# Decay attention with a softplus feed-forward layer on one core: from unit 9 on, scores follow the preceding unit's outputs in one TensorE event

## The chip, the cores and the metric

The kernel runs on one core of a Trainium2 chip. The metric is the device time of one execution in microseconds (us); for the kernel before, the median of three runs is 615.9 us (612.82 to 615.99). Profiles are of one execution each, taken by the hardware profiler; their times count from the first instruction of the span.

## The reference

The first half is causal linear attention with a decay for each head, in blocks of 64 positions; the second half is a feed-forward layer with softplus, and no residual connection.

```
B, H, S, D = 4, 8, 768, 64; block = 64
for b in range(S // block):                       # q, k, v of this block: qb, kb, vb
    intra = (qb @ kb.T * Dmask) @ vb              # Dmask[i, j] = lam ** (i - j) for i >= j, else 0
    inter = (qb * lam ** (pos + 1)) @ kv_state
    out[b] = intra + inter
    kv_state = lam ** block * kv_state + (kb * lam ** (block - 1 - pos)).T @ vb
x = out as (3072 tokens, 512)
h = x @ w_in                                      # 512 -> 2048
y = softplus(h) @ w_out                           # 2048 -> 512
```

## The kernel before

**Tiling of the attention.** The sequence is cut into six chunks (NCH) of 128 positions, two blocks of 64. The heads are cut into four pairs (NP). A *unit* g is one chunk and one pair, with all four batches: 24 units, g = 4c + p. Its q, k and v come in one buffer of 8 KB a partition, att, by two loads on the queue of SyncE (`load_upto`, L80). Keys and queries lie there twice where both layouts are needed; k and v are stored back to front in a block, so the decay products need no more than a scale for each row.

A unit has two bursts of small fp32 matmuls, all 64 by 64, four of which sit beside each other in the array:

- *scores* (`scores_of`, L428, `mm_scores`, L289): the products of k and q into one PSUM bank (x, L299) and the contribution of the decayed keys and v to the state into another (y, L301); 64 matmul records. VectorE then masks x (`mask_scores`, L323, L326) and updates the states from y with four instructions (`update_states`, L353, L331).
- *outputs* (`mm_out`, L307): state times decayed query (L314) and v times masked scores (L318) into a two-bank tile z; 64 records. ScalarE then takes the high half of the result (`x_high`, L361, L363) and VectorE the low half (`x_low`, L368, L370): x is kept as a sum of two rounded parts, and each product of the feed-forward layer takes three matmuls.

Ahead of the scores ScalarE makes the decayed keys (`k_decay`, L269, L277) and VectorE the decayed queries (`q_decay`, L279, L284).

**The feed-forward layer.** A chunk has 512 tokens. Its work is cut into 16 slices f of the hidden 2048. For a step s = 16c + f the first layer (`mlp1`, L389, L398) accumulates twelve matmuls 128x512 into one of two PSUM banks of tag "h"; ScalarE takes softplus of it and rounds it, VectorE takes the rest (`chain_act`, `chain_hi`, `chain_lo`, L377 to L387); and four steps later (LAG) the second layer (`mlp2`, L403, L415) adds twelve matmuls into the four banks of tag "o" of that chunk. At a chunk's last step the four banks are copied out (L421) and stored (L423).

**PSUM.** Eight banks: four of tag "o", two of tag "h", and one two-bank tile of tag "t" (`work`, L66), which scores (x and y) and outputs (z) use in turn.

**SBUF.** A pool of 21 buffers of 8 KB ("b8", L48) holds loaded units, raw weights, converted weights (16 for the rest of the run), x and the output tiles. A pool of four buffers of 2 KB ("b2", L54) holds, from unit 4 on, the decayed keys and queries and the masked scores.

**What sets the order.** The schedule is manual: each engine executes its instructions in the order in which the program traces them. The first steps are a list written out by hand (L453 to L463). Then a loop over s runs from 4 to 99 (L473 to L509). In a step, the decay products of a unit whose scores come in the next step stand first, then softplus of step s-1, weight conversion while there is any, then on TensorE the second layer of step s-4, the scores of a unit if `scores_at` has one for this step, the outputs of a unit if `outs_at` has one, and the first layer of step s; and at the end loads, on SyncE's queue. Units 4 to 7 have their scores at steps 3, 6, 9 and 12, units 8 to 23 at steps 17, 21, ... 77, each with its outputs two steps later:

```
scores_at = {3 * n + 3: NP + n for n in range(NP)}
scores_at.update({4 * n + 1 + NF: 2 * NP + n for n in range(NG - 2 * NP)})
outs_at = {s + 2: g for s, g in scores_at.items()}
```

At the end of a step with scores of unit g, `load_upto(g + 2)` issues the load of unit g+1, which waits until a buffer is free.

**The diagonal.** In the first chunk the state passes from one block to the next through a matmul with a diagonal matrix (`carry_states`, L342, L346), kept in a tile of its own, `diag` (L181). The set-up buffer `spare` (L131), one of the 21, holds the ramps from which masks and powers are made, among them `begins` (L149).

Of the kernel before, what the change touches and what calls it, by code (L numbers as in the profile page):

```python
# [7 lines left out]
F32 = mybir.dt.float32  # L8
# [6 lines left out]
B, H, S, D = 4, 8, 768, 64  # L15
C = 128
T = 64
NCH = S // C
NP = H // 2
NG = NCH * NP  # L20
DM = H * D
DFF = 2048
NF = DFF // 128
LAG = 4
# [7 lines left out]
def decay_attention_softplus_ffn(  # L32
# [7 lines left out]
    nc = tc.nc  # L40
    ctx.enter_context(tc.manual_schedule())
    cp = ctx.enter_context(tc.tile_pool(name="cp", bufs=1))
    sb = ctx.enter_context(tc.tile_pool(name="sb", bufs=2))
# [8 lines left out]
        return sb.tile(shape, dt, tag="b4", bufs=7, name=name)  # L52

    def t2(shape, dt, name):  # L54
        return sb.tile(shape, dt, tag="b2", bufs=4, name=name)

    def tl(shape, dt, name):
        return sb.tile(shape, dt, tag="bl", bufs=1, name=name)
# [7 lines left out]
    def work(name):  # L66

        return ps.tile([128, 2, 512], F32, tag="t", bufs=1, name=name)

    def bank(name):  # L70
        return ps.tile([128, 512], F32, tag="h", bufs=2, name=name)
# [8 lines left out]
    def load_upto(n):  # L80
        for g in range(len(units), min(n, NG)):
            t = t8([128, 2, 2, 512], F32, f"att{g}")
            for major in range(2):
                nc.sync.dma_start(out=t[:, major], in_=att[g // NP, g % NP, :, major])  # L84
            units.append(t)

    def part(g, major, kind):
        return units[g][:, major, kind].rearrange("q (b t d) -> q b t d", b=B, t=2)
# [7 lines left out]
    def kt_of(g):  # L96
        return part(g, 1, 0)

    def vt_of(g):
        return part(g, 1, 1)  # L100


    w_order = [(f, 0) for f in range(LAG)]
# [41 lines left out]
    for s in range(2):  # L145
# [7 lines left out]
        out=begins[0], in_=ramp.rearrange("q (o i) -> q o i", o=1).broadcast_to([128, H, T]), scalar=0.0,  # L153
# [24 lines left out]
    nc.gpsimd.iota(  # L178
        off[half(1)], pattern=[[1, T]], base=0, channel_multiplier=-1, allow_small_or_imprecise_dtypes=True
    )  # L180
    diag = cp.tile([128, H, T], F32, name="diag")  # L181
    nc.vector.scalar_tensor_tensor(
        out=diag[half(1)], in0=off[half(1)].rearrange("q (o i) -> q o i", o=1).broadcast_to([64, H, T]), scalar=0.0,
        in1=lam_c[half(1)].rearrange("q (h o) -> q h o", o=1).broadcast_to([64, H, T]),
# [84 lines left out]
    def k_decay(g):  # L269
        kd = kds[g] = own(g, 0, "kd")  # L270
        if g == 0:
            w = rp1[:, heads(g)].rearrange("q (o t w) -> q o t w", o=1, w=1).broadcast_to([128, B, 2, D])
            nc.vector.tensor_mul(out=kd, in0=kt_of(g), in1=w)
            return
        for t in range(2):
            h = heads(g).start + t
            nc.scalar.activation(kd[:, :, t], kt_of(g)[:, :, t], AF.Copy, scale=rp1[:, h : h + 1])  # L277

    def q_decay(g):  # L279
        qd = qds[g] = own(g, 1, "qd")  # L280
        r = hi if first_chunk(g) else slice(0, 128)
        eng = nc.gpsimd if g < 2 else nc.vector
        w = lp[r, heads(g), :].rearrange("q (o t) i -> q o (t i)", o=1).broadcast_to([r.stop - r.start, B, 2 * T])
        eng.tensor_mul(  # L284
            out=qd[r].rearrange("q b t i -> q b (t i)"), in0=q_of(g)[r].rearrange("q b t i -> q b (t i)"), in1=w
        )


    def mm_scores(g, x, y):  # L289
        q, k, kd, v = q_of(g), k_of(g), kds.pop(g), vt_of(g)  # L290
        if first_chunk(g):

            nc.tensor.matmul(y[lo], lhsT=warm[hi, :64], rhs=warm[hi], start=True, stop=False)
        for b in range(B):
            for t in range(2):
                cols = slice((2 * b + t) * 64, (2 * b + t + 1) * 64)
                for s in range(2):
                    r = half(s)
                    nc.tensor.matmul(x[r, cols], lhsT=k[r, b, t], rhs=q[r, b, t], start=True, stop=True)  # L299
                    if s == 0 or not last_chunk(g):  # L300
                        nc.tensor.matmul(  # L301
                            y[half(1 - s), cols], lhsT=kd[r, b, t], rhs=v[r, b, t],
                            start=s == 0 or not first_chunk(g), stop=s == 0 or not first_chunk(g),
                        )


    def mm_out(g, w):  # L307
        a, qd, v, st = aa.pop(g), qds.pop(g), vt_of(g), states[g]
        for b in range(B):
            cols = slice(b * 64, b * 64 + 64)  # L310
            for s in range(1 if first_chunk(g) else 0, 2):
                r = half(s)
                for t in range(2):
                    nc.tensor.matmul(w[half(t), s, cols], lhsT=st[r, b, t], rhs=qd[r, b, t], start=True, stop=False)  # L314
            for s in range(2):
                r = half(s)
                for t in range(2):
                    nc.tensor.matmul(  # L318
                        w[half(t), s, cols], lhsT=v[r, b, t], rhs=a[r, b, t],
                        start=s == 0 and first_chunk(g), stop=True,  # L320
                    )

    def mask_scores(g, x):  # L323
        a = aa[g] = own(g, 2, "a")
        m = mask[:, heads(g), :].rearrange("q (o t) i -> q o t i", o=1).broadcast_to([128, B, 2, T])
        nc.vector.tensor_mul(out=a, in0=x.rearrange("q (b t i) -> q b t i", b=B, t=2), in1=m)  # L326
# [26 lines left out]
    def update_states(g, y):  # L353
        u = y.rearrange("q (b t e) -> q b t e", b=B, t=2)
        st = states[g]
        decayed(g, st[hi], st[lo], lo, u[hi])
        if not last_chunk(g):
            states[g + NP] = th([128, B, 2, D], F32, f"st_{g + NP}")
            decayed(g, states[g + NP][lo], st[hi], hi, u[lo])

    def x_high(g, w):  # L361

        nc.scalar.copy(  # L363
            out=x_of(g // NP, g % NP)[:, 0].rearrange("q (b s i) -> q s b i", b=B, s=2),
            in_=w[:, :, 0:256].rearrange("q s (b i) -> q s b i", b=B),
        )

    def x_low(g, w):  # L368
        x = x_of(g // NP, g % NP).rearrange("q n (b s i) -> q n s b i", b=B, s=2)
        nc.vector.tensor_sub(  # L370
            out=x[:, 1], in0=w[:, :, 0:256].rearrange("q s (b i) -> q s b i", b=B), in1=x[:, 0]
        )
# [30 lines left out]
    def mlp2(ss):  # L403
        c = ss[0] // NF
        ends = ss[-1] % NF == NF - 1
        if ss[0] % NF == 0:
            o_tiles[c] = [obank(f"o{c}_{b}") for b in range(B)]
        if ends:
            ob = t8([128, B, 512], F32, f"ob{c}")
        for b in range(B):  # L410
            for s in ss:
                f = s % NF
                g, w = g_tiles[s], w_of(f, 1)
                for n, (i, j) in enumerate(((0, 0), (0, 1), (1, 0))):
                    nc.tensor.matmul(  # L415
                        o_tiles[c][b], lhsT=g[:, i, b * 128 : (b + 1) * 128], rhs=w[:, j],
                        start=f == 0 and n == 0, stop=f == NF - 1 and n == 2,
                    )
            if ends:
                copy = nc.vector.tensor_copy if b % 2 else nc.scalar.copy  # L420
                copy(out=ob[:, b], in_=o_tiles[c][b])  # L421
                queue = nc.scalar if c == NCH - 1 and b % 2 == 0 else nc.sync
                queue.dma_start(out=out[b * S + c * C : b * S + (c + 1) * C, :], in_=ob[:, b])  # L423
# [4 lines left out]
    def scores_of(g):  # L428
        w = work(f"w{g}")
        mm_scores(g, w[:, 0], w[:, 1])  # L430
        mask_scores(g, w[:, 0])
        update_states(g, w[:, 1])


    xy, z = {}, {}
# [30 lines left out]

    last = NCH * NF
    scores_at = {3 * n + 3: NP + n for n in range(NP)}  # L470
    scores_at.update({4 * n + 1 + NF: 2 * NP + n for n in range(NG - 2 * NP)})
    outs_at = {s + 2: g for s, g in scores_at.items()}
    for s in range(LAG, last + LAG):  # L473
        if s + 1 in scores_at:
            k_decay(scores_at[s + 1])
            q_decay(scores_at[s + 1])
        if s - 1 < last:
            chain_act(s - 1)
            chain_hi(s - 1)
            chain_lo(s - 1)  # L480
        old, new = w_group(s - 1), w_group(s)
        if old:
            w_hi(*old)
        if new:
            w_scale(*new)
            w_round(*new)
        if old:
            w_lo(*old)
        if new:
            w_shift(*new)  # L490
            w_sign(*new)
            w_add(*new)
        if s == last + LAG - 2:
            mlp2([s - LAG, s - LAG + 1])
        elif s - LAG < last - 1:
            mlp2([s - LAG])
        if s in scores_at:
            scores_of(scores_at[s])
        if s in outs_at:
            g = outs_at[s]  # L500
            w = work(f"z{g}")
            mm_out(g, w)
            x_high(g, w)
            x_low(g, w)
        if s < last:
            mlp1(s)
        w_load(2 * s + (8 if s < 9 else 6))
        if s in scores_at:
            load_upto(scores_at[s] + 2)  # L509


def _layout(q, k, v, lam, w_in, w_out):
# [37 lines left out]
```

## Time and profile before

| | |
|---|---|
| runs | 612.82, 615.90, 615.99 us; median 615.9 us |
| profiled execution | 613.46 us |
| its span | 611.7 us |
| mean granted TensorE clock | 0.992 |
| first layers, L398 | 1152 matmul records, 284.1 us busy |
| second layers, L415 | 1152 matmul records, 276.6 us busy |
| loads of units, L84 | 48 of 512 KB, 5.2 us from issue to landing (median) |

A row of a group gives line, engine, operation, tiles and shapes, the number of instructions, then busy time and the mean time of one in ns, then the engine's idle time just before them and what ended it. PE is TensorE's matmuls, PEld its weight loads, DVE is VectorE, ACT ScalarE, SPq the queue of SyncE. An fp32 matmul of 64 by 64 appears as two records. Matmuls are pipelined, and the recorded end of one is modelled; what a stretch costs is read from starts, or from the chain, whose pieces follow each other without overlap.

### The profile page before, as it was taken

Reading aid. Unit: us, or ns where it says so; the run is one execution under the profiler, and the core shown is the slowest. Engines: PE = TensorE matmul, PEld = TensorE weight load, DVE = VectorE, ACT = ScalarE, POOL = GpSimd, SP = SyncE. Lnnn points to the kernel's source line nnn. Section 1 sums busy time; section 2 is a strip of 40 time slices with the busy share of each in tenths; the row PEclk is TensorE's granted clock in tenths of the full one; section 3 lists DMA queues with packets and bytes.
Section 4 is the critical chain, followed back from the end, with each engine's and each line's share of the span. In section 5 each row is a group of like instructions: output and inputs, shape, how many; then the busy total and the mean of one; then the engine's idle time right before and its main releaser. Section 6 shows DMA issues by size and latency. Waiting matters only on the chain.

```text
span 611.7 us, 11745 instructions
## 1 busy us (share of the span) xinstructions
PE 602.8 (99%) x5289; PEld 488.5 (80%) x5289; DVE 226.7 (37%) x336; ACT 211.8 (35%) x340; POOL 4.6 (1%) x11
## 2 busy tenths in 40 slices
PE   8999999999999999999999999999999999999997
PEld 5677888888888888888888888888888888888886
DVE  7689999843321233223213322222222211210111
ACT  3677777723222224122222232212312221322121
POOL 3000000000000000000000000000000000000000
PEclk9699999999999999999999999999999999999999
DMA  8995324213110033020030320012302000100001
GB/s 297 406 407 215 107 86 138 102 39 138 33 39 1 1 138 115 25 70 2 1 138 28 112 70 1 1 39 100 138 2 70 1 0 1 70 1 1 1 0 69
DMA packets 15169, 48.98 MB, mean 80 GB/s; under 512 B 1808, under 2 KB 1808, under 8 KB 15120
## 3 DMA queue, kind: packets, MB, share of 16 engines
q1 hardware_dynamic: 14832, 47.72, 21.5%
q8 instruction: 41, 0.67, 0.4%
q10 hardware_dynamic: 288, 0.52, 0.2%
q14 instruction: 8, 0.07, 0.0%
HBM read 41.95 MB, written 6.29 MB: 79 GB/s over the span
## 4 chain that ended last, share of the span: by engine, by line
PE 91%; DMA 6%; DVE 1%; SPq 1%; ACT 0%; issue 0%; ACTq 0%; DVEq 0%
PE o L415 42%; PE h L398 42%; DMA att<-in_att 4%; PE w L299 3%; DMA raw<-in_wts 3%; PE z L314 2%; PE z L318 2%; PE w L301 1%; SPq L84 0%; DVE c L217 0%; DVE w L230 0%; DVE c L223 0%; SPq L118 0%; ACT w L226 0%; DVE ob L421 0%; DVE qd L284 0%
## 5 line engine op out<-in xcount | busy, mean ns | idle before, releaser
L398 PE MATMUL h<-x,w 128*128 128x512 f32 x1152 | 284.1, 395 | 0.0
L415 PE MATMUL o<-w,g 128*128 128x512 f32 x1152 | 276.6, 389 | 1.1 <-DVE w L230 0.8
L415 PEld LDWEIGHTS o<-w,g 128*128 128x128 f32 x1152 | 216.1, 188 | 46.7 <-DVE w L230 1.1
L398 PEld LDWEIGHTS h<-x,w 128*128 128x128 f32 x1152 | 213.1, 188 | 47.7 <-issue 1.1
L387 DVE TENSOR_TENSOR g<-l,g 128x512 fp32r<-128x512 f32 x96 | 66.3, 691 | 284.5 <-ACT g L383 284.4
L379 ACT ACTIVATE l<-h 128x512 f32<-128x512 f32 x96 | 57.2, 596 | 307.4 <-PE h L398 304.8
L383 ACT CAST g<-l 128x512 fp32r<-128x512 f32 x96 | 59.6, 621 | 3.1
L331 DVE SCALAR_TENSOR_TENSOR st<-st,lam_c,w 64x256 f32<-64x256 f32 x72 | 31.7, 480 | 0.8
L370 DVE TENSOR_TENSOR x<-z,x 128x512 fp32r<-128x512 f32 x24 | 16.6, 690 | 38.5 <-ACT x L363 38.5
L363 ACT CAST x<-z 128x512 fp32r<-128x512 f32 x24 | 14.0, 583 | 39.5 <-PE z L318 39.4
L299 PEld LDWEIGHTS w<-att 64*64 64x64 f32 x640 | 20.4, 134 | 7.0 <-issue 6.0
L326 DVE TENSOR_TENSOR a<-w,mask 128x512 f32<-128x512 f32 x20 | 13.8, 690 | 29.8 <-PE w L301 22.4
L277 ACT ACTIVATE kd<-att,rp 128x256 f32<-128x256 f32 x40 | 18.1, 503 | 14.4 <-DMA att<-in_att 14.4
L299 PE MATMUL w<-att 64*64 64x64 f32 x640 | 23.1, 221 | 0.0
L301 PE MATMUL w<-att,kd 64*64 64x64 f32 x576 | 23.0, 221 | 0.0
L314 PEld LDWEIGHTS z<-qd,st 64*64 64x64 f32 x640 | 17.0, 134 | 7.0 <-issue 7.0
L205 ACT ACTIVATE c<-raw 128x1024 f32<-128x1024 f32 (+1 forms) x19 | 19.0, 1001 | 7.4 <-DMA raw<-in_wts 7.4
L230 DVE TENSOR_TENSOR w<-c,w 128x1024 fp32r<-128x1024 f32 (+1 forms) x19 | 20.0, 1054 | 2.8 <-ACT w L226 2.7
L226 ACT CAST w<-c 128x1024 fp32r<-128x1024 f32 (+1 forms) x19 | 17.4, 913 | 10.7 <-DVE c L223 8.1
L223 DVE CUSTOM_DVE_ANT_0 c<-raw,c 128x2048 uint16<-128x2048 uint16 (+1 forms) x19 | 20.1, 1058 | 2.4
L314 PE MATMUL z<-qd,st 64*64 64x64 f32 x640 | 20.9, 224 | 0.0
L301 PEld LDWEIGHTS w<-att,kd 64*64 64x64 f32 x576 | 20.3, 134 | 0.0
(47 smaller groups left out, 206.6 us busy)
## 6 DMA issues: line engine op xcount, KB each, us to landing
att<-in_att SPq DMA_DIRECT2D x48, 512.0 KB, 5.2
raw<-in_wts SPq DMA_DIRECT2D x32, 512.0 KB, 10.2
out_dram<-ob SPq DMA_DIRECT2D x22, 256.0 KB, 2.1
out_dram<-ob ACTq DMA_DIRECT2D x2, 256.0 KB, 2.0
lam_b<-in_lam SPq DMA_DIRECT2D x1, 4.0 KB, 2.6
```

What stands on the lines that cost most here:

```text
L205: nc.scalar.activation(c.bitcast(F32), raw_at(ks, 1).bitcast(F32), AF.Copy, scale=2.0**-112)
L223: nc.vector.tensor_add(out=c, in0=c, in1=raw_at(ks, 0))
L230: nc.vector.tensor_sub(out=w[:, 1], in0=conv.pop(ks[0]).bitcast(F32), in1=w[:, 0])
L299: nc.tensor.matmul(x[r, cols], lhsT=k[r, b, t], rhs=q[r, b, t], start=True, stop=True)
L301: nc.tensor.matmul(y[half(1 - s), cols], lhsT=kd[r, b, t], rhs=v[r, b, t], start=s == 0 or not first_chunk(g), stop=s == 0 or not first_ch ...
L314: nc.tensor.matmul(w[half(t), s, cols], lhsT=st[r, b, t], rhs=qd[r, b, t], start=True, stop=False)
L331: nc.vector.scalar_tensor_tensor(out=to[:, :, t], in0=of[:, :, t], scalar=lam_c[r, h : h + 1], in1=u[:, :, t], op0=ALU.mult, op1=ALU.add,)
L379: nc.scalar.activation(l_tiles[s], h_tiles.pop(s), AF.Softplus)
L383: nc.scalar.copy(out=g_tiles[s][:, 0, :], in_=l_tiles[s])
L387: nc.vector.tensor_sub(out=g[:, 1, :], in0=l_tiles.pop(s), in1=g[:, 0, :])
L398: nc.tensor.matmul(h_tiles[s], lhsT=w[:, i, cs], rhs=x[:, j, :], start=p == 0 and n == 0, stop=p == NP - 1 and n == 2,)
L415: nc.tensor.matmul(o_tiles[c][b], lhsT=g[:, i, b * 128 : (b + 1) * 128], rhs=w[:, j], start=f == 0 and n == 0, stop=f == NF - 1 and n == 2,)
```

## The change

From unit 9 on, the scores of unit g are traced in the step in which unit g-1 has its outputs, s = 4g - 17, two steps earlier than before. The outputs stay at their steps. In such a step TensorE has: the second layer of step s-4; the outputs of g-1 into the two-bank tile; the scores of g into the two banks of tag "h" (new tiles x and y); the second layer of step s-3, which is left out of the next step; and the first layer of s. The first layer of s+1 then follows the one of s directly. Behind the outputs and scores, VectorE masks the scores, updates the states and takes the low half of x of g-1; ScalarE takes the high half and then copies v of unit g into a 2 KB buffer (`keep_values`), which the outputs of g read later, so that the unit's load buffer is not read after its scores. Unit 8 keeps its scores at step 17 and gets such a copy too; unit 23 keeps its outputs at step 79 and gets none. Loads are issued at the end of steps with scores, as before. The "b2" pool has five buffers instead of four, and `diag` loses its own tile: it is written into `begins[0]`, in the set-up buffer.

```
     def t2(shape, dt, name):
-        return sb.tile(shape, dt, tag="b2", bufs=4, name=name)
+        return sb.tile(shape, dt, tag="b2", bufs=5, name=name)
...
+    values = {}
+
     def vt_of(g):
-        return part(g, 1, 1)
+        return values[g] if g in values else part(g, 1, 1)
+
+    def keep_values(g):
+        v = t2([128, B, 2, D], F32, f"v_{g}")
+        nc.scalar.copy(out=v, in_=part(g, 1, 1))
+        values[g] = v
...
-    diag = cp.tile([128, H, T], F32, name="diag")
+    diag = begins[0]
...
     scores_at = {3 * n + 3: NP + n for n in range(NP)}
-    scores_at.update({4 * n + 1 + NF: 2 * NP + n for n in range(NG - 2 * NP)})
     outs_at = {s + 2: g for s, g in scores_at.items()}
+    scores_at[NF + 1] = 2 * NP
+    both_at = {4 * g - 17: g for g in range(2 * NP + 1, NG)}
+    outs_at[4 * NG - 17] = NG - 1
+    units_at = {**scores_at, **both_at}
     for s in range(LAG, last + LAG):
-        if s + 1 in scores_at:
-            k_decay(scores_at[s + 1])
-            q_decay(scores_at[s + 1])
+        if s + 1 in units_at:
+            k_decay(units_at[s + 1])
+            q_decay(units_at[s + 1])
...
-        elif s - LAG < last - 1:
+        elif s - LAG < last - 1 and s - 1 not in both_at:
             mlp2([s - LAG])
         if s in scores_at:
             scores_of(scores_at[s])
+            if scores_at[s] == 2 * NP:
+                keep_values(2 * NP)
+        if s in both_at:
+
+            g = both_at[s]
+            w, x, y = work(f"z{g - 1}"), bank(f"x{g}"), bank(f"y{g}")
+            mm_out(g - 1, w)
+            mm_scores(g, x, y)
+            mask_scores(g, x)
+            x_high(g - 1, w)
+            update_states(g, y)
+            x_low(g - 1, w)
+            if g < NG - 1:
+                keep_values(g)
+            mlp2([s + 1 - LAG])
...
-        if s in scores_at:
-            load_upto(scores_at[s] + 2)
+        if s in units_at:
+            load_upto(units_at[s] + 2)
```

## The prediction

> **What bounds the kernel now.** I read the page's busy shares first, then the chain of work that ended last, whole and then for two events, then the timeline of TensorE inside those events, and last the groups, waits and loads that could take over.
>
> ```profile
> span 611.7 us, 11745 instructions
> PE 602.8 (99%) x5289; PEld 488.5 (80%) x5289; DVE 226.7 (37%) x336; ACT 211.8 (35%) x340; POOL 4.6 (1%) x11
> ...
> PE 91%; DMA 6%; DVE 1%; SPq 1%; ACT 0%; issue 0%; ACTq 0%; DVEq 0%
> ```
>
> TensorE carries 91% of the chain; the 6% of DMA is the start-up. VectorE and ScalarE are idle for over 60% of the span. What is worth something is therefore TensorE time, and a busy share of 99% says nothing of how well that time is used. So here is the chain around one scores event and one outputs event of the same unit (start, length, what):
>
> ```profile
> 295.91 2.72 PE o L415 x12
> ...
> 299.72 2.95 PE h L398 x12
> 302.67 2.72 PE o L415 x12
> 305.39 2.72 PE h L398 x12
> 308.11 2.72 PE o L415 x12
> 310.82 0.28 PE z L314 x8
> 311.10 0.12 PE z L318 x8
> 311.22 0.12 PE z L314 x8
> ...
> 311.80 0.12 PE z L318 x8
> 311.92 2.95 PE h L398 x12
> 314.87 2.72 PE o L415 x12
> ...
> 494.89 2.95 PE h L398 x12
> 507.09 2.95 PE h L398 x12
> ```
>
> A layer of twelve 512-column matmuls takes 2.72 us, first or second, whichever stands before it. With an event between two of them it is otherwise. From the second layer at 295.91 to that at 302.67 pass 6.76 us, which is two layers of 2.72 and 1.32 us; from 308.11 to 314.87 pass 6.76 us again. So an event costs 1.32 us, scores or outputs, and the last two rows, 12.20 us apart like 299.72 and 311.92, show the same step (four layers and 1.32) at the end of the stretch.
>
> The outputs event shows what the 1.32 us are made of. Its 64 small records come in eight groups. Each group after the first takes 0.12 us (from 311.10 to 311.92 seven groups take 0.82, 0.117 each); the first takes 0.28, 0.16 more; and the layer behind the event takes 2.95, 0.23 more than 2.72. So 8 times 0.117, or 0.93 us, is work, and 0.39 us (0.16 going in, 0.23 coming out) is paid once for each event.
>
> ```profile
> 298.66 0.22 PE L299 MATMUL w<-att 64*64 64x64 f32 x1
> ...
> 299.50 0.22 PE L301 MATMUL w<-att,kd 64*64 64x64 f32 x1
> 299.65 3.02 PE L398 MATMUL h<-x,w 128*128 128x512 f32 x12
> ...
> L299 PEld LDWEIGHTS w<-att 64*64 64x64 f32 x640 | 20.4, 134 | 7.0 <-issue 6.0 <-DVE x L370 0.7 <-DVE g L387 0.4
> L314 PEld LDWEIGHTS z<-qd,st 64*64 64x64 f32 x640 | 17.0, 134 | 7.0 <-issue 7.0
> ```
>
> The scores event agrees: after its first four records, 60 start between 298.66 and 299.50, 14 ns apart, and 0.15 us pass before the big matmuls start. The weight loads show the entry from the other side: they idle 7.0 us over 20 events of either kind, 0.35 us each, released mostly by "issue", no other engine. The fixed cost comes where the shape in use goes from 128*128 to 64*64 and back.
>
> **What the change does to TensorE.** Units 9 to 23 have their scores at step 4g-17 instead of 4g-15, in the event in which unit g-1 has its outputs anyway. Of the 30 events (scores of 9 to 23, outputs of 8 to 22) 15 are left, each of 128 records; scores of 4 to 8 and outputs of 4 to 7 and of 23 stay alone. No matmul is added or taken away. Two events cost 2 times 1.32, or 2.64 us; a merged one 0.39 + 2 times 0.93, or 2.25. That saves 0.39 us in each, 15 times: 5.9 us. The condition is that outputs pass into scores without a switch. No row before shows these two next to each other at full clock; the nearest is from the start-up, where scores pass into the 64*64 carry of the states:
>
> ```profile
> 27.11 0.31 PE L299 MATMUL x<-att 64*64 64x64 f32 x1
> ...
> 28.60 0.31 PE L299 MATMUL x<-att 64*64 64x64 f32 x1
> ...
> 28.62 0.31 PE L301 MATMUL y<-att,own 64*64 64x64 f32 x1
> 28.73 1.11 PE L346 MATMUL y<-st,diag 64*64 64x256 f32 x4
> ```
>
> Other line, other operands, other width, and the next start comes 0.11 us after, which is the step between groups of four there (14 steps from 27.11 to 28.60, 0.106 each). Inside the outputs event L314 and L318 alternate too, at the even 0.12. So I take nothing for the passage; the ends are 0 and the whole 0.39, a full switch. In the other direction I allow one group of eight, 0.12, counted to the wrong side, so 0.51 saved at most, 7.6 us in all.
>
> The moved second and first layers cost what they cost: order does not show in the 2.72.
>
> **What must be ready.** The scores of a merged event leave the two-bank work tile to the outputs and take both banks of the first layer's sums. New waits can only be these; queued behind a late one on TensorE would be everything. The rows:
>
> ```profile
> L326 DVE TENSOR_TENSOR a<-w,mask 128x512 f32<-128x512 f32 x20 | 13.8, 690 | 29.8 <-PE w L301 22.4 <-PE w L299 7.4
> L370 DVE TENSOR_TENSOR x<-z,x 128x512 fp32r<-128x512 f32 x24 | 16.6, 690 | 38.5 <-ACT x L363 38.5
> L363 ACT CAST x<-z 128x512 fp32r<-128x512 f32 x24 | 14.0, 583 | 39.5 <-PE z L318 39.4
> ...
> 299.79 0.69 DVE L326 TENSOR_TENSOR a<-w,mask 128x512 f32<-128x512 f32 x1 [1.87 <-PE w L301]
> 300.49 1.79 DVE L331 SCALAR_TENSOR_TENSOR st<-st,lam_c,w 64x256 f32<-64x256 f32 x4
> 302.70 0.60 ACT L379 ACTIVATE l<-h 128x512 f32<-128x512 f32 x1 [5.51 <-PE h L398]
> ```
>
> Count from the start of the second layer before a merged event. It ends at 2.72, outputs at 2.72 + 0.16 + 0.93 = 3.81, scores at 4.74, the second layer behind at 4.74 + 2.95 = 7.69, the first of the two first layers at 10.41. Scores need the bank that softplus of the preceding step reads: softplus starts 0.03 after its layer (302.67 to 302.70) and takes 0.60, so it is free at 0.63, 3.2 us early. The masking starts 0.07 after scores and takes 0.69: the first bank is free at 5.50, needed at 7.69. The four state updates end 1.79 later at 7.29: the second bank is needed at 10.41, 3.1 us later. The low half of x follows them on VectorE and ends at 7.98; where a chunk begins at the next step its first layer starts at 10.41. The nearest slack is 2.2 us. Softplus of the first of the two layers finds its bank needed again only after another first and a second layer, 5.44 us.
>
> Copying v of units 8 to 22 adds 15 copies on ScalarE; the nearest row is L363, 0.583 us for 128x512, 8.7 us in all on an engine that works 211.8 us. It stands behind the high half of x and ahead of a softplus that waits for a layer ending at 10.41: hidden, about 5 us of cover. Were the cover gone, it would delay only that softplus.
>
> Loads: the copy lets a unit's load buffer go after its scores instead of its outputs, and each load from unit 10 on is issued two steps earlier, in the same order against the output stores.
>
> ```profile
> SPq L84 <- PE z L318: 151.4, 7, 22.4
> ACT kd L277 <- DMA att<-in_att: 14.4, 3, 4.8
> ...
> 312.02 2.32 SPq L84 DMA_DIRECT2D att<-in_att  x4
> 317.36 0.91 ACT L277 ACTIVATE kd<-att,rp 128x256 f32<-128x256 f32 x2 [4.79 <-DMA att<-in_att]
> ...
> DMA to landing us min/median/max: 3.3/5.2/11.2
> ```
>
> Before, the loads wait for outputs (151.4 us), and three times ScalarE waits for a load that was issued only at the end of the outputs just before it (312.02, used at 317.36). Nothing on the chain waited for that. After, a load is issued with three steps, 16.3 us, before its decay product, against 11.2 for the slowest landing. This cover grows, so I cost it at zero.
>
> The diagonal now lies in the set-up buffer, which is held until its last reader:
>
> ```profile
> L346 PE MATMUL y<-st,diag x16: 376/376/631, 13.8 to 36.1; 64*64 64x256 f32 x16
> ...
> L318 PE MATMUL z<-own,att x128: 218/218/366, 11.4 to 31.6; 64*64 64x64 f32 x128
> ...
> 38.66 1.56 SPq L84 DMA_DIRECT2D att<-in_att  x2
> ```
>
> That reader starts at 36.1 and takes 0.63 at most. Buffers are handed out in the order in which they come free, so each load issued meanwhile moves up by one in that line; the last that it can be given before 36.7 are those of the first units, read last at 31.6, and from the load at 38.66 on the held one is free again. I cost it at zero; a converted weight takes the held one later.
>
> **The sum.** The profiled execution took 613.46 us with its span of 611.7. Less 5.9 it is 607.6. The runs shown are 612.82, 615.90 and 615.99: with the profiled one, two lie near 613 and two near 616. From the median of 615.9 the sum is 610.0. I take the middle of the two, 608.8.
>
> **The rivals.** *Slower: the small matmuls run out of instructions.* An event has 64 records and as many weight loads; merged, twice that without a big matmul, behind which the sequencer gains a lead. Should that lead last for one half only, the other half goes at the rate of supply. The slowest steady pace of the trace is the start-up's, 56 records from 27.11 to 28.60, 26.6 ns each against 14.5; 64 records more at that pace cost 0.77 us extra, the merged event 3.02 instead of 2.64, 15 times 0.38 or 5.7 us: 619.2 by the profiled execution, 621.6 by the median. It decides against the change from 20.6 ns a record (1.32 us over 64). For it: no row shows over 64 at full clock. Against it: the pace does not flag within the 64, and the start-up's follows a slower clock (the second slice of the page, 15.3 to 30.6 us):
>
> ```profile
> PEclk9699999999999999999999999999999999999999
> ```
>
> I give it a chance of 0.08.
>
> The Trainium skill, "TensorE: Matmul & The Clock Gate", section "Wait — 56ns, not 53.3ns?", states a floor of about 25 ns between starts of matmuls however short they are, and its opening table an engine queue of 64. An estimate by that floor for the second half alone would be 64 times 10.5 ns, 0.67 us, hence 4.2 us slower in all. The trace disagrees with the floor: the 60 starts above lie 14 ns apart, so the sum keeps 14.5.
>
> *No gain: outputs to scores is a switch of its own.* Both are 64*64, but on other rows and banks, and the merged event pays 0.39 inside: 613.5 to 615.9. The passage at 28.73 speaks against it. Chance 0.06.
>
> *No gain: a bank comes late.* VectorE runs behind by over 2.2 us and the first layer waits for its bank; a wait of 0.39 us eats all, 613.5 to 615.9. For it: all the small work of two units now falls into one step. Against it: its total there is 0.69 + 1.79 + 0.69 in two steps of 5.44. Chance 0.07.
>
> **The numbers.** The forecast has 0.79, the rivals 0.08, 0.06 and 0.07. A measurement of this kernel tells about 0.5%, 3.1 us, from no change, and the saving is nearly twice that. The range goes from 605.2 (612.82 less 7.6) to 614.0, which takes in no gain at the lower level of the runs; no gain at the upper level and the slower case stay out. Faster 0.79, same 0.13, slower 0.08.
>
> **What would show it.** In the chain of the changed kernel from the second layer ahead of a merged event to the second first layer behind it pass three layers (8.16 us) and 2.25 us, with sixteen groups of eight, all but the first of them 0.12, and 2.95 for the layer behind. Idle of the weight loads at L299 falls from 20 to 5 events' worth, about 1.8 us, while that at L314 stays. The waits of decay products for loads are gone in the middle. Wrong are the steps if small records start over 20 ns apart in the second half, if a gap stands between outputs and scores, or if first layers get idle time released by VectorE.

## The result and the profile after

The changed kernel takes 609.26 us (median of six runs, 607.41 to 611.60), the kernel before 614.23 us in its six (612.22 to 615.99). The ratio is 0.992, 95% interval 0.9896 to 0.9945: 0.8% faster. The profiled execution took 611.60 us; it is the slowest of the six; what goes with that is told below.

The page of the changed kernel, lines on the span, the engines and the chain:

```profile
span 609.8 us, 11757 instructions
PE 601.6 (99%) x5289; PEld 491.8 (81%) x5289; DVE 226.9 (37%) x336; ACT 219.8 (36%) x355; POOL 4.1 (1%) x11
...
PE 95%; DVE 3%; ACT 1%; issue 0%; DMA 0%; DVEq 0%; ACTq 0%
```

TensorE has the same 5289 matmul records and is 99% busy again. The share of busy time cannot show what was won; the chain can. Here it is around one merged event (start, length, what), then two later rows in step with it:

```profile
303.55 2.72 PE o L423 x12
306.27 2.72 PE h L406 x12
308.99 2.72 PE o L423 x12
311.71 0.28 PE z L322 x8
311.98 0.12 PE z L326 x8
...
312.68 0.12 PE z L326 x8
312.80 0.04 PE x L307
...
313.72 0.03 PE x L307
313.76 2.95 PE o L423 x12
316.70 5.44 PE h L406 x24
322.14 2.72 PE o L423 x12
...
337.79 2.95 PE o L423 x12
```

Second layer to second layer takes 4.77 us, from 308.99 to 313.76: 2.72 of matmuls and 2.05 of event, and the layer behind pays 0.23 more. A merged event costs 2.28 us. Its outputs take 1.09 (311.71 to 312.80), 0.16 over eight groups of 0.117, and its scores 0.96. Four steps take 24.03 us (313.76 to 337.79), where twice 12.20, two steps each, made 24.40 before.

What the whole change is worth on TensorE shows between two rows that every profile has: the first first layer that comes right behind an event in the steady part, and the last four second layers. Before:

```profile
54.40 2.95 PE h L398 x12
...
597.08 10.89 PE o L415 x48
```

And in the changed kernel:

```profile
57.77 2.95 PE h L406 x12
...
595.24 10.89 PE o L423 x48
```

The stretch shrinks from 542.68 to 537.47 us, by 5.21. But it begins 3.37 us later. The windows of 15.3 us (columns: length, busy time of PE, PEld, DVE, ACT, POOL, then the granted TensorE clock and DMA) show what goes with it. Before, then changed:

```profile
15.30:30.60 15.30, 13.93 (x242) 9.56 (x242) 10.50 (x18) 10.38 (x20) 0.00 (x0) 0.67 1.03 406
30.60:45.90 15.30, 15.30 (x168) 11.96 (x168) 12.33 (x22) 11.62 (x21) 0.00 (x0) 1.00 1.03 407
```

```profile
15.30:30.60 15.30, 13.93 (x240) 9.42 (x239) 10.41 (x17) 10.12 (x20) 0.00 (x0) 0.60 1.03 406
30.60:45.90 15.30, 15.30 (x151) 11.28 (x151) 9.22 (x16) 8.99 (x16) 0.00 (x0) 0.73 1.03 408
```

In the third window the granted clock was 1.00 before and 0.73 in this execution. The later start belongs to this execution and not to the change: another execution of the same kernel, below, starts the stretch at 54.35.

### The profile page after: what moved, and what is told of

Read it like the earlier page. It is cut to its first block, busy times and chain, and to the rows that moved or that the text cites. A ratio compares the mean times of both kernels' runs of the same rounds, so it can differ in the third digit from the quotient of the medians.

```text
span 609.8 us, 11757 instructions
## 1 busy us (share of the span) xinstructions
PE 601.6 (99%) x5289; PEld 491.8 (81%) x5289; DVE 226.9 (37%) x336; ACT 219.8 (36%) x355; POOL 4.1 (1%) x11
## 4 chain that ended last, share of the span: by engine, by line
PE 95%; DVE 3%; ACT 1%; issue 0%; DMA 0%; DVEq 0%; ACTq 0%
PE o L423 43%; PE h L406 42%; PE z L322 3%; PE x L307 2%; PE z L326 2%; PE y L309 1%; PE y L354 1%; PE w L307 1%; DMA lam_b<-in_lam 0%; DVE w L238 0%; DVE spare L190 0%; DVE st L339 0%; PE y L301 0%; ACT w L234 0%; DVE g L395 0%
## 5 line engine op out<-in xcount | busy, mean ns | idle before, releaser
L406 PE MATMUL h<-x,w 128*128 128x512 f32 x1152 | 280.2, 394 | 0.0
L406 PEld LDWEIGHTS h<-x,w 128*128 128x128 f32 x1152 | 217.3, 190 | 48.0 <-issue 1.5
L334 DVE TENSOR_TENSOR a<-x,mask 128x512 f32<-128x512 f32 x15 | 10.4, 692 | 36.3 <-PE y L309 26.5
L307 PE MATMUL x<-att 64*64 64x64 f32 x608 | 23.7, 229 | 0.0
L339 DVE SCALAR_TENSOR_TENSOR st<-st,lam_c,y 64x256 f32<-64x256 f32 x52 | 22.9, 480 | 0.8
L307 PEld LDWEIGHTS x<-att 64*64 64x64 f32 x608 | 21.7, 144 | 1.4 <-issue 1.4
L225 DVE SCALAR_TENSOR_TENSOR c<-raw,c 128x1024 uint32<-128x1024 uint32 (+1 forms) x19 | 20.1, 1056 | 0.6
L217 ACT ACTIVATE raw<-raw 128x1024 uint32<-128x1024 uint32 (+1 forms) x19 | 18.8, 991 | 0.0
```

The lines of the kernel that those rows point to most:

```text
L225: nc.vector.scalar_tensor_tensor(out=c, in0=raw_at(ks, 1), scalar=0x80000000, in1=c, op0=ALU.bitwise_and, op1=ALU.bitwise_or)
L339: nc.vector.scalar_tensor_tensor(out=to[:, :, t], in0=of[:, :, t], scalar=lam_c[r, h : h + 1], in1=u[:, :, t], op0=ALU.mult, op1=ALU.add,)
L406: nc.tensor.matmul(h_tiles[s], lhsT=w[:, i, cs], rhs=x[:, j, :], start=p == 0 and n == 0, stop=p == NP - 1 and n == 2,)
```

## The experiments

**The merged event taken apart.** All of the change stays but the neighbourhood of outputs and scores:

```
-            mm_out(g - 1, w)
             mm_scores(g, x, y)
             mask_scores(g, x)
-            x_high(g - 1, w)
             update_states(g, y)
-            x_low(g - 1, w)
-            if g < NG - 1:
-                keep_values(g)
             mlp2([s + 1 - LAG])
+            w = work(f"z{g - 1}")
+            mm_out(g - 1, w)
+            x_high(g - 1, w)
+            x_low(g - 1, w)
+            if g < NG - 1:
+                keep_values(g)
```

> All of the change stays (early loads, copies of v, the five buffers, the diagonal in the set-up buffer, scores two steps earlier, two second and two first layers in a row), but the merged event is taken apart: scores, then the second layer, then the outputs, then the first layer. Theory (a fixed cost is paid each time TensorE goes into small matmuls and out again, 0.36 us by the profile after): 15 more times 0.36, 5.4 us more than the changed kernel, so level with the kernel before, ratio 1.000, and the chain from the first whole first layer to the last four second layers 542.9 us instead of 537.5. Rival (the gain comes from what else moved: earlier loads, order of the layers): it stays with the changed kernel, ratio 0.992, 537.5 us.

It took 613.43 us against 613.48 before, ratio 1.0004 (0.9985 to 1.0022). The chain of its profile, the two rows of the stretch:

```profile
55.99 2.94 PE h L406 x12
...
598.67 10.89 PE o L423 x48
```

542.68 us, to the hundredth the stretch of the kernel before. The whole gain hangs on the two bursts (scores and outputs) standing next to each other. The earlier loads, the copies of v, the fifth small buffer, the place of the diagonal and the order of the layers are together worth nothing in this stretch, and by the ratio at most 0.2% of the whole.

**One matmul between them.** Of the second layer that follows the event, the first matmul is put between outputs and scores:

```
             mm_out(g - 1, w)
+            mlp2_part(s + 1 - LAG, range(1))
             mm_scores(g, x, y)
...
-            mlp2([s + 1 - LAG])
+            mlp2_part(s + 1 - LAG, range(1, 12))
```

> As the changed kernel, but one matmul of the second layer (of its twelve) stands between outputs and scores, the other eleven behind. Theory (a fixed cost for each passage between the two kinds of matmul, whatever lies between): 5.4 us more than the changed kernel, 542.9 us in the stretch, as with the whole layer between. Rival (the cost grows with the work that has to run out ahead of an event, so that one matmul has little to run out): under 2 us more, below 539.5 us.

It took 614.80 us (before 613.48), ratio 1.001 (0.9992 to 1.0028).

```profile
56.81 2.95 PE h L406 x12
...
599.19 10.89 PE o L423 x48
```

542.38 us: 4.91 more than the merged event, 0.33 each of the 15. A single matmul between the bursts costs almost as much as twelve (0.35, from 5.21 over 15), so the cost belongs to the passage and not to what has to run out ahead of it.

**Scores twice.** `mm_scores(g, x, y)` stands twice in each merged event, and `mm_scores` reads `kds[g]` in place of `kds.pop(g)`. The extra scores are the same work again. An event then has 192 records in place of 128; the last four, whose scores have 48 records, have 160 in place of 112.

> As the changed kernel, but the scores of each merged event are computed twice, the second time over the first, so an event has 192 records in place of 128. Theory (only the records count, at an even pace): 15 times 0.93 to 0.96, 14.0 to 14.4 us more than the changed kernel, 551.5 to 551.9 us in the stretch. Rival (the supply of instructions runs out in a long event): the last 64 at up to 26.6 ns, 25 us more, 563 us.

It took 632.84 us, ratio 1.0293 (1.0258 to 1.0329) to before. The stretch of its chain is 618.19 less 56.91, 561.28 us, 23.8 more than the changed kernel: far over the 14.4 of the theory and close to the rival's 25, yet not as the rival had it. The chain (first and last rows of one event, and the two later ones that show an undisturbed step):

```profile
246.86 2.99 PE o L423 x12
...
271.88 2.94 PE o L423 x12
...
296.75 0.03 PE x L307
296.81 0.03 PE x L307
296.85 1.62 issue
298.47 3.02 PE o L423 x12
```

Where nothing disturbs it, four steps take 25.02 us (246.86 to 271.88), 0.98 more than the usual 24.04 of the changed kernel, for 64 records more: the pace does not sag. But in other events TensorE stops altogether. Here it stands for 1.62 us behind the last record, with nothing to wait for but "issue"; 15 times 0.98 make 14.7, and 9.1 us are left for stops like this. The waits of TensorE on "issue" (for what, total, times, longest) count eight of them, seven inside the burst and one behind it:

```profile
PE y L309 <- issue: 4.2, 4, 1.4
PE x L307 <- issue: 1.7, 3, 0.8
PE o L423 <- issue: 1.6, 1, 1.6
```

In the window from 294 to 299 of this profile the queue of the instructions moved just one block, in the fifteenth of 40 slices, about 295.8, in the event and a microsecond ahead of the stop; over the run that queue moved 48 blocks of 16 KB, and 41 in the changed kernel, which fits TensorE's instructions in blocks of 256 (two for each of 6185 and 5289 records):

```profile
DMA  0000000000000060000000000000000216599494
...
q8 instruction: 1, 0.02, 1.6%
```

The other stops lie the same way. The packets in the trace give for each of the eight one block whose transfer begins 0.95 to 2.05 us after the first record of the event and takes 0.9 to 1.4 us; the first matmul behind the stop starts 1.3 to 1.5 us after that transfer has ended. In the seven events without a stop the next block's transfer begins 2.05 to 3.17 us after the first record. So the stops end with the arrival of instructions, as far as a trace can show that: the rival's mechanism exists, but begins behind the length of the merged event. With 128 records, neither profile of the changed kernel has a stop in the stretch; with 160 all four events have one, with 192 four of eleven.

The Trainium skill, "Runtime: NRT & Kernel Launch", section "Instruction fetch mechanics", says that instructions come in 16 KB blocks of 256 and that fetching them is hidden, since the sequencer issues more slowly than blocks arrive. The block size agrees with 0.79 MB in 48 blocks; hidden it was not in the event shown, with its 384 instructions of 64 by 64 work.

**The changed kernel again**, beside the others.

> The changed kernel once more, beside the others on one chip. Theory: ratio 0.992 to the kernel before and 537.5 us in the stretch of the chain; what its time differs by from run to run lies ahead of the stretch, in the first 50 us, where the granted clock differs. Rival (the change itself delays the start, through the held set-up buffer): the stretch begins 3 us later than before in this profile too, at 57.8 us instead of 54.4.

It took 608.03 us (607.23 to 611.76), ratio 0.9919 (0.989 to 0.9948). Its chain and its second and third window:

```profile
54.35 2.95 PE h L406 x12
...
591.83 10.89 PE o L423 x48
```

```profile
15.30:30.60 15.30, 12.44 (x272) 8.37 (x271) 11.12 (x18) 10.65 (x20) 0.00 (x0) 0.89 1.02 406
30.60:45.90 15.30, 14.66 (x138) 11.39 (x139) 11.71 (x21) 11.35 (x20) 0.00 (x0) 1.00 1.03 407
```

The stretch is 537.48 us, 0.01 from the first profile. It begins at 54.35, as before the change (54.40), so the 3.37 us of the first profile are not a price of the change. That the held set-up buffer costs nothing at all this pair does not show, as the clocks differ (0.89 in the second window, 0.67 before). The kernel with the event taken apart holds that buffer too and is level with the kernel before within 0.2%, some 1.3 us.

In every profile of this case the granted clock is 1.00 outside the second and third window, and the two stretches of the changed kernel agree to 0.01 us. So what spreads a kernel's profiles lies ahead of the stretch, and it goes with the clock granted from 15.3 to 45.9 us: by the trace the clock is at half there for 20.5 us in the first profile of the changed kernel, for 3.4 in the second. Which of the two brings the other about is not shown. Of other runs only the mean clock is known. The first six runs of the changed kernel fall in line: 1.000 for 607.41 us, 0.991 for 607.98 and 608.35, 0.988 for 610.17 and 610.32, 0.982 for 611.60. The order is a loose one: two runs of the kernel before took 612.63 and 614.03 us at the same 0.994.

**Shape or type?** The small matmuls differ from the layers in two things, 64 by 64 for 128 by 128 and fp32 for fp32r. Four kernels put one matmul of 64 columns between second and first layer in steps without events; its product is not read. There are 38 such places, not 37 as the expectations have it. Each of the four kernels ran once (616.65, 622.14, 616.82 and 630.18 us, against 612.77 for the kernel before), so the stretch of the chain is compared, which two profiles of the changed kernel gave alike to 0.01 us.

```
+        if 20 < s < 95 and s % 4 in (1, 2):
+            extra = work(f"extra{s}")
+            nc.tensor.matmul(
+                extra[0:64, 0, 0:64], lhsT=w_of(0, 0)[0:64, 0, 0:64],
+                rhs=w_of(0, 0)[0:64, 0, 0:64], start=True, stop=True,
+            )
         if s < last:
             mlp1(s)
```

This is the one of 64 by 64 in fp32r; for 128 by 128 the three sizes of rows and weight columns are 128, for fp32 the operands come from `mask`.

> The changed kernel with one more matmul between second and first layer in 37 steps without events: 64 columns, fp32r, 128 by 128, the type and shape of the layers. Its product is not used. Both theories: only its columns, 0.03 to 0.10 us each, 1 to 4 us in the stretch of the chain.

> The same 37 places, the matmul fp32r as in the layers but 64 by 64 as in the events; its product is not used. Theory (the shape decides): 0.39 us more in each than a 128 by 128 one, 14 us. Rival (the type, fp32 against fp32r, decides): as the 128 by 128 one, within 2 us.

> The same 37 places, the matmul fp32 as in the events but 128 by 128 as in the layers; its product is not used. Theory (the shape decides): 0.1 to 0.2 us each for its two records, 4 to 8 us, no more. Rival (the type decides): 0.39 us on top, 18 to 22 us.

> The same 37 places, the matmul fp32 and 64 by 64, as in the events; its product is not used. Both theories: 0.39 us and its own 0.06 to 0.12, 16 to 19 us; more than shape or type alone only if each of them has a share.

| kernel | stretch of the chain, us | over the changed kernel's 537.47 | each of 38 |
|---|---|---|---|
| fp32r, 128 by 128 | 600.29 - 57.48 = 542.81 | 5.34 | 0.14 |
| fp32r, 64 by 64 | 605.78 - 54.08 = 551.70 | 14.23 | 0.37 |
| fp32, 128 by 128 | 600.46 - 53.55 = 546.91 | 9.44 | 0.25 |
| fp32, 64 by 64 | 613.80 - 58.09 = 555.71 | 18.24 | 0.48 |

The rows of the chain for the first two:

```profile
57.48 2.95 PE h L406 x12
...
600.29 10.89 PE o L423 x48
```

```profile
54.08 2.94 PE h L406 x12
...
605.78 10.89 PE o L423 x48
```

Only the last of the four stays in its expected size: 5.34 us stand against 1 to 4, 8.9 between the first two against 14, 9.44 against 4 to 8, 18.24 against 16 to 19. Yet shape and type can be told apart. The shape adds 0.23 us with either type (0.37 less 0.14, 0.48 less 0.25). The type adds 0.11 with either shape, and it brings a second record of each matmul. So the passage is one of shape, as the theory said, but smaller than its 0.39 on top: of the 0.37 that a lone small matmul costs, 0.14 are paid by a matmul of the layers' own shape and type too. The weight loads, idle time last but for its releasers, say the same. The groups of the added weight loads, fp32r 128 by 128, fp32 128 by 128, then fp32r 64 by 64 and fp32 64 by 64:

```profile
L534 PEld LDWEIGHTS extra<-w 128*128 128x128 f32 x38 | 7.1, 188 | 1.5
```

```profile
L534 PEld LDWEIGHTS extra<-mask 128*128 128x128 f32 x76 | 14.3, 188 | 2.9
```

```profile
L534 PEld LDWEIGHTS extra<-w 64*64 64x64 f32 x38 | 4.9, 129 | 13.4 <-issue 9.5 <-DVE qd L292 3.9
```

```profile
L534 PEld LDWEIGHTS extra<-mask 64*64 64x64 f32 x76 | 7.1, 131 | 13.4 <-issue 9.5 <-DVE qd L292 3.9
```

13.4 us over 38 are 0.35 each, for either type: the same 0.35 that the events showed before the change (7.0 over 20). With the layers' shape it is 0.04 for each load (1.5 over 38, 2.9 over 76). So in these runs the next weights are loaded ahead while a matmul runs as long as the shape stays, and not when it goes over to 64 by 64. The Trainium skill, "TensorEngine Tiling (Array Packing)", section "Key Properties", says that a change of the tiling mode drains the engine while a change of the tile does not. These runs agree: going to another shape and back costs 0.23 us more than staying, and outputs to scores, inside one shape, cost some hundredths. What makes up the rest of an event's 0.35 us, these runs do not separate.

**Further in the same direction.** The early units merged as well, by the step table alone:

```
-    scores_at[NF + 1] = 2 * NP
-    both_at = {4 * g - 17: g for g in range(2 * NP + 1, NG)}
+    scores_at = {3: NP}
+    outs_at = {}
+    both_at = {3 * g - 9: g for g in range(NP + 1, 2 * NP + 1)}
+    both_at.update({4 * g - 17: g for g in range(2 * NP + 1, NG)})
```

> The changed kernel taken further: the outputs of units 4 to 7 are merged with the scores of units 5 to 8, at steps 6, 9, 12 and 15 (outputs of 4 to 6 and 7 one step later, scores of 8 two steps earlier), in the stretch where VectorE is 94% busy with the weights. Theory: four more merged events, 1.4 us less than the changed kernel, ratio 0.990 to before. Rival (there the banks or the weights of the second layer come late, as VectorE has no slack): first or second layers wait, and it is slower than the changed kernel, by up to 4 us.

It took 618.07 us, ratio 1.0069 to before (1.0044 to 1.0093), 9 to 10 us slower than the changed kernel; the expectation had 4 at most. The waits of its profile (engine and line, for what, total, times, longest):

```profile
PE h L406 <- DVE a L334: 4.1, 4, 1.0
PE o L423 <- DVE w L238: 3.4, 8, 0.7
```

And VectorE's timeline ahead of the first layer of step 9:

```profile
84.88 1.23 DVE L231 CUSTOM_DVE_ANT_0 c<-raw,c 128x2048 uint16<-128x2048 uint16 x1
86.02 0.68 DVE L334 TENSOR_TENSOR a<-x,mask 128x512 f32<-128x512 f32 x1
```

In all four new events the first layer waits for the masking, which has given up the two-bank tile for the first layer's own bank and stands behind the conversion of weights on VectorE; and the second layer, moved up by a step, waits for weights that VectorE has only just converted. The two waits are 7.5 us; in the two profiles of the changed kernel the same two come to 0.2 and 0.8. So they are most of the loss. This is the rival "a bank comes late", true where VectorE has no slack and untrue from unit 9 on.

## Why the prediction was right

*The fixed cost.* Predicted 0.39 us an event and 5.9 in all; the stretch gave 5.21, 0.35 each of the 15, and the medians 4.97. The mechanism was right; the term that was sized too high is the merged event, 2.25 predicted and 2.28 measured in the event shown, and up to 0.08 more in some others (four steps take 24.02 to 24.11 us). Its scores take 0.96 where eight even groups would take 0.93: the passage from outputs to scores was costed at nothing and takes some hundredths. The first of the two "no gain" rivals, a full switch inside, is refuted by the same row: no first group of 0.28 at 312.80. One count was wrong without harm. The scores of units 20 to 23 have only 48 records, because the program leaves out half of the state products in the last chunk, so four merged events have 112 records and not 128; from the first record to the layer behind they take 2.04 to 2.07 us, the others 2.05 to 2.11.

*The idle of the weight loads.* Predicted 1.8 us for the scores events that stay alone, and an unchanged 7.0 for outputs. The groups of the changed kernel:

```profile
L322 PEld LDWEIGHTS z<-qd,st 64*64 64x64 f32 x640 | 17.0, 134 | 7.0 <-issue 7.0
...
L307 PEld LDWEIGHTS w<-att 64*64 64x64 f32 x160 | 5.1, 134 | 1.8 <-issue 1.1 <-DVE x L378 0.4 <-DVE g L395 0.4
```

Both are as predicted. The merged scores are in no idle group at all.

*The banks.* Predicted slack 2.2 us for the first bank and about 3 for the second. VectorE in the event shown above:

```profile
313.79 0.69 DVE L334 TENSOR_TENSOR a<-x,mask 128x512 f32<-128x512 f32 x1 [2.79 <-PE y L309]
314.51 1.79 DVE L339 SCALAR_TENSOR_TENSOR st<-st,lam_c,y 64x256 f32<-64x256 f32 x4
316.33 0.69 DVE L378 TENSOR_TENSOR x<-z,x 128x512 fp32r<-128x512 f32 x1
```

The first bank is free at 314.48 and needed at 316.70, 2.2 us later; the second at 316.30 and needed 2.72 after 316.70, 3.1 later. No first layer waits.

*Copies and loads.* The 15 copies of v took 0.62 us each, 9.3 in all (predicted 8.7), hidden. The wait of the decay products for loads went from 14.4 us to 0.9, and the experiment with the event taken apart shows that this was worth nothing, as costed.

*The diagonal.* Costed at zero, and nothing seen: 54.35 against 54.40 at the start of the stretch, at clocks that differ, and level within 0.2% in the runs of the kernel with the event taken apart.

*The slower rival.* It had a chance of 0.08 for the wrong length: instructions do run out, at 160 and 192 records an event and not at 128, and as a stop, not as a slower pace.

*The level.* That 608.8 and 609.26 lie 0.5 us apart is luck. The forecast is the middle of two sums, 607.6 and 610.0; the measured median is the middle of six runs of which three lie at 607.4 to 608.4 and three at 610.2 to 611.6, and six other runs of the same kernel gave 608.03. What the prediction had right is the saving and where it comes from. What goes with the levels, the clock granted from 15.3 to 45.9 us, it did not see.

## What to carry to other kernels

Where small tiled matmuls interleave with full-size ones on a TensorE that never rests, count the passages: the cost of one is read from the chain as the step between two layers less the even work, and neighbours of one shape share it. Before moving work next to its like, check whose buffers then become common, in the busiest stretch of the engine that empties them and not on average. And a burst can be made too long: past some length, here between 128 and 160 records, the supply of instructions decides.

## What the runs showed of the hardware that was not expected

- A burst of 128 small records (256 instructions with their weight loads) in 2.05 us ran without a stop. With 192 records in 3 us or more, or 160, 8 of 15 events stopped, for up to 1.62 us, until 1.3 to 1.5 us after the transfer of an instruction block had ended. The spared events lie such that their next block's transfer begins 2.05 us or more behind their first record; no run moved an event against the blocks to test this.
- A single 64-column matmul of the layers' own shape and type between two layers costs 0.14 us, not the 0.03 to 0.10 expected.
- The granted clock between 15.3 and 45.9 us differs from execution to execution (0.73 and 1.00 in the third window of the same kernel), and with it the start of the stretch, 57.77 and 54.35 us.
- 48 records of scores take as long as 64: the merged events of 112 records last 2.04 to 2.07 us, those of 128 records 2.05 to 2.11.
